# Copies of finished PSUM banks one step earlier, a strict turn of two banks, a fourth W_out step beside the attention units, and a new order at the loop's ends

## The chip, the core and the metric

The kernel runs on one NeuronCore of a Trainium2 chip. Its engines work in parallel, each through its own queue in order: TensorE (PE, with its weight loads as PEld), VectorE (DVE), ScalarE (ACT), GpSimd (POOL), and SyncE (SP), which here only starts DMAs. They wait for each other by semaphores. The metric is the device time of one execution in microseconds (us), the median of three runs.

## The reference

```python
scores = (q @ k.transpose(0, 1, 3, 2)) / sqrt(64)      # q, k, v: 8 batches x 8 heads x 576 x 64
scores = where(row // 64 >= col // 64, scores, -1e9)   # causal by blocks of 64
attn = exp(scores - max); attn = attn / (sum(attn) + 1e-9)
x = (attn @ v).transpose(0, 2, 1, 3).reshape(4608, 512)
h = x @ w_in                                           # 512 x 2048
out = (h * sigmoid(h)) @ w_out                         # 2048 x 512
```

## The kernel before

**Two halves of a number.** Inputs of the two FFN products are split into a rounded part ("hi", an ACT copy to fp32r) and a remainder ("lo", a subtraction), and each product is three fp32r matmuls. W_in and W_out arrive as 64-bit words and are turned into fp32 by hand: `load` (DMA), `rebias` (ACT), `bits:0` to `bits:2` (DVE). W_out has eight steps `t0` to `t7` of two half-steps each (`o0` to `o15`). A step then gets four ACT copies (`hi:0` to `hi:3`), three differences of its quarters (`x:0` to `x:2`) and four remainders (`lo:0` to `lo:3`). The first NTA steps go to a pool `ta` and leave `lo` and `x` to POOL alone; later ones use DVE for two `lo` and one `x`, and lie in pools that exist only when the attention's buffers have been given back (`all.attended`).

**The stages.** First (to about 80 us) the weights of W_in and the first two row blocks of the attention, in a packed form of their own. Then the loop: 64 units (batch, head), in 32 pairs `d0` to `d31`, with the remaining rows of the attention. Beside it run the steps of the first FFN product (`ffn1`), 160 in all, each into one PSUM bank `h`. After the loop the rest of them, then the second FFN product (`Item.prod`) until the end.

**A pair in the loop.** `run:0` and `run:1` interleave the scores of this pair with attn @ v of the pair two before (`score` and `pv`). The latter goes to two banks: `U` (`r` = 1) and one of the two banks of pool `pH`, where it is called `u` (`r` = 0). `half` (ACT, L795) copies `U` to SBUF, `fold` (DVE, L799) adds `u` to it and so frees `u`. POOL's `mult`, ACT's `x_hi` and POOL's `x_lo` make of it the input of later FFN steps. Then four FFN steps of two tokens `ffn` each take PE (L1067, 12 matmuls of 448 columns a step). Meanwhile DVE finds the maxima (`max`, L655, L704), their largest over partition groups goes through ACT's small copies (`gather`, `spread`) and DVE (`top`, `wide`), DVE subtracts (`sub`, L730, L733), ACT takes `exp` (L737), POOL adds up the row sums (`add`, L744 to L752), DVE reduces them (`sums`, L655 into `dj`), ACT gathers `dj` (`sums_g`, L664), POOL adds (`sums_m`, L808 to L812), and DVE inverts (`inverse`).

**The FFN's banks.** A step's bank `h` comes from `pH`, which has two buffers, and so do `u` and, later, two banks of the second product. A finished step is copied to SBUF by ACT (`keep`, L1073) and goes to DRAM by a DMA (`save`, L1078). The pool gives the next tile the buffer that, in the order below, is the first to be released.

**The order** of all this is written out by hand as a list of tokens, ORDER. Each token puts its instructions at the end of its engine's queue. `ffn`, `keep` and `save` take the next step of their own lists, so that a `keep` in the list belongs to the oldest step not yet copied. With steps counted, the tokens of one pair that concern PE and the banks read, where f81 is step 81, f81a and f81b its two halves, and K81 its copy:

```
d18.run:0 K79 d18.run:1 d16.half f81a d16.fold f81b f82a K80 f82b f83a K81 f83b f84a K82 f84b  d19.run:0 K83 ...
```

So K81 stands in the list behind the first half of step 83, two steps after its own.

Of the kernel before, what the change touches and what calls it, by code (L numbers as in the profile page):

```python
# [107 lines left out]
d0.fold t1.x:0 u5.load_v u8.load u9.load u5.max:0 d0.mult u4.top ffn u5.ones u5.max:1 u4.spread u5.max:2 d0.x_hi ffn u4.wide
keep d0.x_lo u5.gather u4.sub:0 save ffn t1.hi:1 u5.top u4.sub:1 u5.spread t1.x:1 u3.sums u4.exp:0 ffn u4.sub:2 t1.lo:1 keep
u5.wide d1.sums_g save u5.sub:2 ffn u4.exp:1 d1.sums_m u4.exp:2 u5.sub:0 u5.exp:2 u5.sub:1 d3.run:0 keep u4.add:0 d1.inverse  # L110
u5.exp:0 save u5.exp:1 u4.add:1 t1.hi:2 u4.add:2 d3.run:1 u4.add:3 d1.half u5.add:0 u4.sums u6.max:0 u5.add:1 ffn u6.max:1
u6.load_v u6.ones u7.load_v u10.load u11.load u6.max:2 u5.add:2 u5.add:3 ffn d1.fold u6.gather u7.max:0 d1.mult u6.top u7.ones
ffn u7.max:1 keep t1.x:2 u7.max:2 u6.spread save ffn u7.gather u6.wide d1.x_hi u6.sub:0 t1.hi:3 ffn d1.x_lo u7.top u6.sub:1 keep
u5.sums u7.spread save t1.lo:3 u6.sub:2 ffn d2.sums_g u7.wide u6.exp:0 d2.sums_m u7.sub:2 u6.exp:1 ffn keep u7.sub:0 u6.exp:2
u7.sub:1 u6.add:0 save ffn u7.exp:0 d2.inverse u7.exp:1 u6.add:1 u7.exp:2 d4.run:0 u6.add:2 keep u6.add:3 save u7.add:0 u6.sums
d4.run:1 d2.half u8.max:0 u7.add:1 u8.max:1 u8.ones u7.add:2 u8.max:2 u7.add:3 u8.gather ffn t1.lo:2 u8.load_v d2.fold u9.load_v
u12.load u13.load u9.max:0 d2.mult u8.top ffn u9.ones u9.max:1 u8.spread u9.max:2 d2.x_hi ffn u8.wide keep d2.x_lo u9.gather
u8.sub:0 save ffn u8.exp:0 u9.top u8.sub:1 u9.spread u7.sums u8.exp:1 ffn u8.sub:2 keep u8.add:0 u9.wide d3.sums_g save u9.sub:2
ffn u8.exp:2 d3.sums_m u9.sub:0 u9.exp:2 u9.sub:1 u9.exp:0 d5.run:0 u8.add:1 keep d3.inverse u9.exp:1 u8.add:2 save u8.add:3
u9.add:0 d5.run:1 u8.sums d3.half u10.max:0 u9.add:1 u10.max:1 u10.ones u10.max:2 u9.add:2 u9.add:3 u10.load_v d3.fold  # L120
u11.load_v u10.gather u14.load u15.load u11.max:0 d3.mult u10.top u11.ones u11.max:1 u10.spread u11.max:2 d3.x_hi u10.wide
u11.gather d3.x_lo u10.sub:0 u11.top u10.exp:0 ffn u10.sub:1 u11.spread u9.sums u10.exp:1 u10.sub:2 ffn d4.sums_g u10.add:0
u11.wide u10.exp:2 u11.sub:2 ffn keep d4.sums_m u11.sub:0 u11.exp:2 save u11.sub:1 ffn u11.exp:0 u11.exp:1 u10.add:1 d4.inverse
d6.run:0 u10.add:2 keep u10.add:3 save u11.add:0 u10.sums d6.run:1 d4.half u12.max:0 u11.add:1 u12.max:1 u12.ones u11.add:2
u12.max:2 u11.add:3 u12.gather ffn u12.load_v d4.fold u13.load_v u16.load u17.load u13.max:0 d4.mult ffn u12.top u13.ones
u13.max:1 u12.spread u13.max:2 ffn keep u12.wide u13.gather save ffn u12.sub:0 d4.x_hi u13.top u12.exp:0 d4.x_lo u12.sub:1 ffn
u13.spread u11.sums keep u12.sub:2 d5.sums_g ffn save u13.wide u12.exp:1 d5.sums_m u13.sub:2 u12.exp:2 ffn u13.sub:0 keep
u13.sub:1 u13.exp:0 u12.add:0 save ffn d5.inverse u13.exp:1 u13.exp:2 u12.add:1 d7.run:0 keep u12.add:2 save u12.add:3 u13.add:0
u12.sums d7.run:1 d5.half u14.max:0 u13.add:1 u14.max:1 u14.ones u13.add:2 u14.max:2 u13.add:3 u14.gather ffn u14.load_v d5.fold
u15.load_v u18.load u19.load u15.max:0 d5.mult ffn u14.top u15.ones u15.max:1 u14.spread u15.max:2 ffn keep u14.wide u15.gather  # L130
save ffn u14.sub:0 d5.x_hi u15.top u14.exp:0 d5.x_lo u14.sub:1 ffn u15.spread u13.sums keep u14.sub:2 d6.sums_g ffn save
u15.wide u14.exp:1 d6.sums_m u15.sub:2 u14.exp:2 ffn u15.sub:0 keep u15.sub:1 u15.exp:0 u14.add:0 save ffn d6.inverse u15.exp:1
u15.exp:2 u14.add:1 d8.run:0 keep u14.add:2 save u14.add:3 u15.add:0 u14.sums d8.run:1 d6.half u16.max:0 u15.add:1 u16.max:1
u16.ones u15.add:2 u16.max:2 u15.add:3 u16.gather ffn u16.load_v d6.fold u17.load_v u20.load u21.load u17.max:0 d6.mult ffn
u16.top u17.ones u17.max:1 u16.spread u17.max:2 ffn keep u16.wide u17.gather save ffn u16.sub:0 d6.x_hi u17.top u16.exp:0
d6.x_lo u16.sub:1 ffn u17.spread u15.sums keep u16.sub:2 d7.sums_g ffn save u17.wide u16.exp:1 d7.sums_m u17.sub:2 u16.exp:2 ffn
u17.sub:0 keep u17.sub:1 u17.exp:0 u16.add:0 save ffn d7.inverse u17.exp:1 u17.exp:2 u16.add:1 d9.run:0 keep u16.add:2 save
u16.add:3 u17.add:0 u16.sums d9.run:1 d7.half u18.max:0 u17.add:1 u18.max:1 u18.ones u17.add:2 u18.max:2 u17.add:3 u18.gather
ffn u18.load_v d7.fold u19.load_v u22.load u23.load u19.max:0 d7.mult ffn u18.top u19.ones u19.max:1 u18.spread u19.max:2 ffn
keep u18.wide u19.gather save ffn u18.sub:0 d7.x_hi u19.top u18.exp:0 d7.x_lo u18.sub:1 u19.spread u17.sums keep u18.sub:2 ffn  # L140
d8.sums_g save u19.wide u18.exp:1 d8.sums_m u19.sub:2 ffn u18.exp:2 u19.sub:0 u19.exp:2 u19.sub:1 d10.run:0 u19.exp:0 u18.add:0
d8.inverse keep u19.exp:1 save u18.add:1 u18.add:2 d10.run:1 u18.add:3 d8.half u19.add:0 u18.sums u20.max:0 u19.add:1 u20.max:1
ffn u20.ones u20.load_v u21.load_v u24.load u25.load u20.max:2 u19.add:2 u19.add:3 ffn d8.fold u20.gather u21.max:0 d8.mult ffn
u20.top u21.ones u21.max:1 keep u21.max:2 u20.spread save ffn d8.x_hi u20.wide u21.gather d8.x_lo ffn u20.sub:0 keep u21.top
u20.exp:0 u20.sub:1 save ffn u21.spread u19.sums u20.sub:2 d9.sums_g ffn u21.wide keep d9.sums_m u20.exp:1 u21.sub:2 save ffn
u20.exp:2 u21.sub:0 u21.exp:2 u20.add:0 u21.sub:1 u21.exp:0 d11.run:0 d9.inverse keep u20.add:1 u21.exp:1 save u20.add:2
u20.add:3 d11.run:1 d9.half u21.add:0 u20.sums u22.max:0 u21.add:1 u22.max:1 u22.ones u22.max:2 u21.add:2 ffn u22.load_v
u23.load_v u26.load u21.add:3 u27.load d9.fold u22.gather ffn u23.max:0 d9.mult u22.top u23.ones u23.max:1 ffn u22.spread
u23.max:2 keep u22.wide d9.x_hi ffn save u23.gather d9.x_lo u22.sub:0 ffn u23.top u22.exp:0 u22.sub:1 keep u21.sums u23.spread
# [1149 lines left out]
```

## Time and profile before

| | |
|---|---|
| Median of 3 runs | 1012.25 us (1011.24 to 1014.05) |
| The profiled execution | 1012.83 us, of which the span from the first to the last instruction is 1011.1 us |
| Mean granted TensorE clock | 0.992 |
| Busy: PE / PEld | 951.9 us (94%) / 825.5 us (82%) |
| Busy: DVE / ACT / POOL | 742.6 (73%) / 640.8 (63%) / 552.6 us (55%) |
| The chain that ended last | PE 74%, DVE 14%, ACT 6% |

How to read it: 59 us of the span are without PE. Which engine a stage waits for is not seen in shares of the whole span, but in the waits of that stage, and in what each engine does within one pair.

### The profile page before, as it was taken

What the parts mean: (1) busy time and instruction counts of PE and PEld (TensorE: products, weight loads), DVE (VectorE), ACT (ScalarE), POOL (GpSimd) and SP (SyncE); (2) the same over time, 40 slices, a digit from 0 to 9 for tenths busy, and PEclk for the clock granted to TensorE, in tenths of its full rate; (3) what the DMA queues carried; (4) which work ended last, traced back from release to release, by engine and by line L of the source; (5) the groups of instructions that cost most, each with busy time, mean ns of one, the idle gap of its engine ahead of it and who ended that gap; (6) DMA issues with size and microseconds to landing.
All of it is one profiled execution on the core that took longest, in us unless ns stands there. A gap on an engine that the chain in (4) does not pass through costs nothing.

```text
span 1011.1 us, 23797 instructions
## 1 busy us (share of the span) xinstructions
PE 951.9 (94%) x8730; PEld 825.5 (82%) x8730; DVE 742.6 (73%) x1518; ACT 640.8 (63%) x1621; POOL 552.6 (55%) x800
## 2 busy tenths in 40 slices
...
GB/s 353 369 170 135 113 97 113 101 116 122 99 130 103 115 120 98 128 98 132 144 118 116 81 61 198 203 205 127 172 163 132 152 137 126 159 132 134 144 81 42
DMA packets 109813, 139.97 MB, mean 138 GB/s; under 512 B 22656, under 2 KB 87168, under 8 KB 109696
## 3 DMA queue, kind: packets, MB, share of 16 engines
...
q8 instruction: 68, 1.11, 0.5%
...
HBM read 91.23 MB, written 47.19 MB: 137 GB/s over the span
## 4 chain that ended last, share of the span: by engine, by line
PE 74%; DVE 14%; ACT 6%; issue 2%; POOL 2%; DMA 1%; SPq 0%; DVEq 0%; ACTq 0%; POOLq 0%
PE h L1067 24%; PE c L1150 19%; PE S L1150 15%; PE u L791 6%; DVE Mx L655 6%; PE S L791 5%; PE SC L791 2%; DVE MR L659 2%; DVE xu L799 2%; ACT g L1073 2%; DVE p L730 2%; ACT m L722 2%; ACT p L737 1%; DMA p<-in_qk_dram 1%; DVE mj L704 1%
## 5 line engine op out<-in xcount | busy, mean ns | idle before, releaser
L1067 PE MATMUL h<-x,wi 128*128 128x448 f32 (+2 forms) x1968 | 425.6, 372 | 49.0 <-DVE xu L799 25.1
L1067 PEld LDWEIGHTS h<-x,wi 128*128 128x128 f32 x1968 | 361.2, 190 | 99.9 <-ACT g L1073 34.9
L1132 POOL TENSOR_TENSOR wi<-raw,wi 128x512 fp32r<-128x512 f32 (+1 forms) x114 | 115.9, 1030 | 148.2 <-ACT wi L1128 106.0
L1150 PE MATMUL c<-tb,wi 128*128 128x256 f32 x663 | 120.2, 276 | 0.0
L737 ACT ACTIVATE p<-p 128x448 f32<-128x448 f32 (+2 forms) x192 | 100.6, 572 | 7.5 <-DVE p L730 6.2
L1150 PEld LDWEIGHTS c<-tb,wi 128*128 128x128 f32 x663 | 102.0, 188 | 0.0
L791 PE MATMUL S<-qk 64*64 64x384 f32 (+1 forms) x512 | 98.6, 516 | 0.0
L1073 ACT COPY g<-h 128x448 f32<-128x448 f32 (+1 forms) x160 | 85.8, 536 | 17.6 <-PE h L1067 11.7
L655 DVE TRANSPOSE_TENSOR_REDUCE dj<-pa 128x14 f32<-128x448 f32 x64 | 40.6, 634 | 76.1 <-POOL pa L752 76.1
L1150 PE MATMUL S<-tb,wi 128*128 128x256 f32 x513 | 94.4, 276 | 0.0
L1095 ACT ACTIVATE raw<-raw 128x1024 f32<-128x1024 f32 x72 | 76.7, 1065 | 16.9 <-DMA raw<-gdb 10.1
L795 ACT COPY xb<-U 128x448 f32<-128x448 f32 x32 | 17.0, 532 | 107.8 <-PE U L791 107.8
L744 POOL TENSOR_TENSOR pa<-p 128x448 f32<-128x448 f32 x64 | 73.5, 1148 | 19.4 <-ACT p L737 12.5
L1150 PE MATMUL c<-ta,wi 128*128 128x256 f32 x519 | 83.8, 276 | 0.0
L747 POOL TENSOR_TENSOR pa<-pa,p 128x256 f32<-128x256 f32 (+1 forms) x128 | 78.1, 610 | 10.0
L791 PE MATMUL U<-p,v 64*64 64x64 f32 (+4 forms) x768 | 79.8, 354 | 0.0
L791 PE MATMUL u<-p,v 64*64 64x64 f32 (+4 forms) x768 | 78.4, 350 | 1.3 <-DVE xu L799 1.3
L1150 PEld LDWEIGHTS S<-tb,wi 128*128 128x128 f32 x513 | 79.2, 188 | 0.0
L1150 PEld LDWEIGHTS c<-ta,wi 128*128 128x128 f32 x519 | 73.3, 188 | 0.0
L730 DVE TENSOR_TENSOR p<-S,MR 128x448 f32<-128x448 f32 (+1 forms) x128 | 71.6, 581 | 1.1
L829 POOL TENSOR_TENSOR x<-xu,x 128x448 fp32r<-128x448 f32 x32 | 37.1, 1159 | 61.2 <-ACT x L826 59.6
L655 DVE TRANSPOSE_TENSOR_REDUCE Mx<-S 128x14 f32<-128x448 f32 (+1 forms) x128 | 69.2, 576 | 0.0
...
## 6 DMA issues: line engine op xcount, KB each, us to landing
gdb<-g SPq DMA_DIRECT2D x128, 224.0 KB, 2.0
...
```

What stands on the lines that cost most here:

```text
L655: nc.vector.tensor_reduce(out=out, in_=in_, axis=AX.X, op=op, apply_transpose=True)
L730: nc.vector.tensor_tensor(out=u.p[:, c : c + w], in0=s[:, :w], in1=u.mb[:, q : q + w], op=ALU.subtract)
L737: nc.scalar.activation(u.p[:, c : c + w], u.p[:, c : c + w], AF.Exp, scale=SCALE)
L744: nc.gpsimd.tensor_tensor(out=u.pa, in0=p[:, :NQ], in1=p[:, ZERO:COLS], op=ALU.add)
L747: nc.gpsimd.tensor_tensor(out=u.pa[:, q : q + w], in0=u.pa[:, q : q + w], in1=p[:, c : c + w], op=ALU.add)
L791: nc.tensor.matmul(o, w, x, start=start, stop=stop)
L829: nc.gpsimd.tensor_tensor(out=u.x[:, 1], in0=u.xu, in1=u.x[:, 0], op=ALU.subtract)
L1067: nc.tensor.matmul(o, w, x, start=half == 0 and i == 0 or f is None and i == 0, stop=(half == 1 or f is None) and i == len(runs) - 1)
L1073: nc.scalar.copy(g, hs.pop(z)[:, :n])
L1095: nc.scalar.activation(u.raw, u.raw, AF.Silu)
L1132: e.tensor_tensor(out=u.goal(1, k), in0=u.source(k), in1=u.goal(0, k), op=ALU.subtract)
L1150: nc.tensor.matmul(o[:, :HD], *runs[k], start=first, stop=u.q == 3 and n == 5, skip_group_check=True)
```

## The change

Nothing that is computed changes. Six edits:

- **Banks.** `pH` becomes two tiles with names of their own, and a new function takes them strictly in turn.
- **Copies.** From step 13 on the copy of each finished step (`keep`, and `save` behind it) stands one step earlier in the list: at every place where K79 stood, K80 stands now, and so on. The places themselves stay.
- **Buffers.** `half` copies straight into the tile that `fold` then adds to in place (tile `xb` is gone). The first NTA steps of W_out take their differences in place (no tile `xs`). The score tile is 64 columns shorter, and its strip of zeros is cleared before the first unit and no longer at the program's start.
- **A fourth W_out step beside the units.** NTA is 4. `t3` (with `o6`, `o7`) moves from behind the loop into the pairs d24 to d29, and `t2` (with `o4`, `o5`) from the pairs d23 to d31 to the pairs d17 to d24.
- **The loop's start.** The tokens of `t0`, `t1`, `o2`, `o3` are spread differently over pairs d0 to d4. Pairs d2 to d5 get three FFN steps each (before 3, 4, 3, 2), and the second half of step 32 changes places with the first half of step 33.
- **The loop's end.** Between the last two `run`s stand two FFN steps, where there was none, and behind `all.attended` come `o8` and `o9`.

```diff
-NTA = 3
+NTA = 4
-COLS = 1472
+COLS = 1408
-FOURS, TWOS, ONES, ZERO, WIDE = 448, 704, 832, 1024, 1088
+FOURS, TWOS, ONES, ZERO, WIDE = 448, 704, 832, 960, 1024
...
-    pH = pool("pH", bufs=2, space=PSUM)
+    pH = pool("pH", space=PSUM)
+    turns = [0]
+
+    def turn(name):
+        turns[0] += 1
+        return pH.tile([P, 512], F32, tag=f"h{turns[0] % 2}", name=name)
...
-    for t in PP:
-        nc.gpsimd.memset(t[:, ZERO:WIDE], 0.0)
...
-                u.sums = sp.tile([P, 4, 256], F32, tag="xs", name="xs")
-                e.tensor_tensor(out=u.sums[:, 0:2], in0=q[:, 1:4:2], in1=q[:, 0:2], op=sub)
+                if u.d < NTA:
+                    u.sums = [q[:, 0:2], q[:, 1:3]]
+                else:
+                    s = sp.tile([P, 4, 256], F32, tag="xs", name="xs")
+                    u.sums = [s[:, 0:2], s[:, 2:4]]
+                e.tensor_tensor(out=u.sums[0], in0=q[:, 1:4:2], in1=q[:, 0:2], op=sub)
...
+            if u.i == 0:
+                for t in PP:
+                    nc.gpsimd.memset(t[:, ZERO:WIDE], 0.0)
...
-            U = u.U[r] = pU.tile([P, 512], F32, tag="U", name="U") if r else pH.tile([P, 512], F32, tag="h", name="u")
+            U = u.U[r] = pU.tile([P, 512], F32, tag="U", name="U") if r else turn("u")
...
-            u.xb = sp.tile([P, NQ], F32, tag="xb", name="xb")
-            nc.scalar.copy(u.xb, u.U[1][:, :NQ])
+            u.xu = sp.tile([P, 512], F32, tag=f"xu{u.k % 2}", name="xu")[:, :NQ]
+            nc.scalar.copy(u.xu, u.U[1][:, :NQ])
...
-            u.xu = sp.tile([P, 512], F32, tag=f"xu{u.k % 2}", name="xu")[:, :NQ]
-            nc.vector.tensor_tensor(out=u.xu, in0=u.U[0][:, :NQ], in1=u.xb, op=ALU.add)
+            nc.vector.tensor_tensor(out=u.xu, in0=u.U[0][:, :NQ], in1=u.xu, op=ALU.add)
...
-            hs[z] = pH.tile([P, 512], F32, tag="h", name="h")
+            hs[z] = turn("h")
...
+    f = queues["ffn"]
+    f[65], f[66] = f[66], f[65]
```

Of ORDER, with the steps counted as above, a pair in the middle, and the loop's end:

```
before  d18.run:0 K79 d18.run:1 d16.half f81a d16.fold f81b f82a K80 f82b f83a K81 f83b f84a K82 f84b  d19.run:0 K83
after   d18.run:0 K80 d18.run:1 d16.half f81a d16.fold f81b f82a K81 f82b f83a K82 f83b f84a K83 f84b  d19.run:0 K84

before  d32.run:0 K135 d33.run:0 d30.half d30.fold f137a d31.half f137b K136 d31.fold f138 K137 all.attended o6.load o7.load
        o6.rebias o6.bits f139a o7.rebias K138 f139b ...
after   d32.run:0 K136 f137a d30.half d30.fold f137b f138a K137 f138b d33.run:0 K138 f139a d31.half d31.fold f139b f140a K139
        f140b K140 all.attended o8.load o9.load f141 f142a K141 o8.rebias f142b o9.rebias f143a K142 f143b ...
```

Where the new tokens of W_out stand in a pair: two or three `bits` behind `inverse`, ahead of `sums` (for `o4` and `o6` the third stands ahead of `fold`); `hi` on ACT ahead of `half`; `lo` and `x` on POOL ahead of `mult`, ahead of `x_lo` or ahead of `sums_m`.

## Rows read from the trace of the kernel before

**Rows 1.** PE's waits, 60 to 180 us: total us, times, longest us
```profile
PE h L1067 <- ACT g L1073: 5.7, 5, 3.1
```

**Rows 2.** PE's waits, 180 to 590 us
```profile
PE h L1067 <- DVE xu L799: 21.3, 26, 1.8
PE h L1067 <- ACT g L1073: 11.1, 22, 0.5
```

**Rows 3.** PE's waits, 590 to 620 us
```profile
PE h L1067 <- ACT g L1073: 5.3, 2, 3.1
PE u L791 <- DVE xu L799: 1.3, 1, 1.3
```

**Rows 4.** Windows: length, busy us of PE, PEld, DVE, ACT, POOL; clock, DMA
```profile
181.24:581.89 400.65, 369.23 (x3588) 289.46 (x3588) 305.82 (x631) 249.25 (x781) 260.69 (x457) 1.00 0.38 115
...
620.00:1011.10 391.10, 387.77 (x3249) 384.75 (x3248) 282.84 (x595) 263.52 (x495) 163.44 (x162) 1.00 0.49 142
```

**Rows 5.** Timeline of PE, pair d18: start, us, what, [idle before <-releaser]
```profile
367.01 0.59 PE L791 MATMUL S<-qk 64*64 64x448 f32 x2
...
372.56 5.08 PE L1067 MATMUL h<-x,wi 128*128 128x448 f32 x24 [0.76 <-DVE xu L799]
378.14 3.08 PE L1067 MATMUL h<-x,wi 128*128 128x448 f32 x14 [0.51 <-ACT g L1073]
```

**Rows 6.** Timeline of DVE, the same pair
```profile
368.04 0.65 DVE L655 TRANSPOSE_TENSOR_REDUCE dj<-pa 128x14 f32<-128x448 f32 x1 [2.62 <-POOL pa L752]
369.55 0.72 DVE L655 TRANSPOSE_TENSOR_REDUCE Mx<-SC 128x16 f32<-128x512 f32 x1 [0.87 <-PE U L791]
...
371.88 0.62 DVE L799 TENSOR_TENSOR xu<-u,xb 128x448 f32<-128x448 f32 x1 [0.23 <-PE u L791]
...
376.98 0.62 DVE L655 TRANSPOSE_TENSOR_REDUCE dj<-pa 128x14 f32<-128x448 f32 x1
...
384.18 0.65 DVE L655 TRANSPOSE_TENSOR_REDUCE dj<-pa 128x14 f32<-128x448 f32 x1 [2.61 <-POOL pa L752]
```

**Rows 7.** Timeline of ACT, the same pair
```profile
369.61 0.53 ACT L795 COPY xb<-U 128x448 f32<-128x448 f32 x1 [3.66 <-PE U L791]
...
374.31 0.53 ACT L1073 COPY g<-h 128x448 f32<-128x448 f32 x1
...
377.56 0.53 ACT L1073 COPY g<-h 128x448 f32<-128x448 f32 x1
378.12 0.66 ACT L664 COPY dj<-dj 32x28 f32<-32x28 f32 x3
```

**Rows 8.** Timeline of POOL, the same pair
```profile
378.86 0.30 POOL L808 TENSOR_TENSOR rt<-dj 32x56 f32<-32x56 f32 x1 [1.49 <-DVE MR L659]
...
383.17 0.98 POOL L752 TENSOR_TENSOR pa<-pa,p 64x128 f32<-64x128 f32 x2
```

**Rows 9.** Timeline of DVE, pair d10, behind a pair with three FFN steps
```profile
242.59 0.67 DVE L655 TRANSPOSE_TENSOR_REDUCE Mx<-SC 128x16 f32<-128x512 f32 x1
...
256.52 0.65 DVE L655 TRANSPOSE_TENSOR_REDUCE dj<-pa 128x14 f32<-128x448 f32 x1 [2.34 <-POOL pa L752]
```

**Rows 10.** Timeline of DVE, between pairs d27 and d28, with W_out work
```profile
527.55 1.11 DVE L563 SCALAR_TENSOR_TENSOR wraw<-wst,wraw 128x512 uint32<-128x512 uint32 x1
```

**Rows 11.** Timeline of POOL, the same pair
```profile
527.31 1.67 POOL L747 TENSOR_TENSOR pa<-pa,p 128x256 f32<-128x256 f32 x2
```

**Rows 12.** Timeline of DVE, first maximum of pairs d2 and d6
```profile
114.74 0.72 DVE L655 TRANSPOSE_TENSOR_REDUCE Mx<-SC 128x16 f32<-128x512 f32 x1 [0.38 <-PE U L791]
...
179.00 0.72 DVE L655 TRANSPOSE_TENSOR_REDUCE Mx<-SC 128x16 f32<-128x512 f32 x1 [3.20 <-PE U L791]
```

**Rows 13.** Timeline of PE at the loop's end
```profile
601.86 9.07 PE L1067 MATMUL h<-x,wi 128*128 128x448 f32 x36 [2.25 <-ACT g L1073]
...
613.98 10.27 PE L1067 MATMUL h<-x,wi 128*128 128x448 f32 x36 [3.06 <-ACT g L1073]
```

**Rows 14.** Windows, as rows 4, right behind the second of these stalls
```profile
614.00:616.00 2.00, 2.00 (x5) 1.80 (x6) 1.86 (x3) 0.84 (x2) 0.73 (x1) 0.50 0.61 154
```

More of the change, by code (lines that the diff above doesn't have):

```diff
@@ L108 @@
[L108 to L149, printed above, removed]
@@ L166 @@
-d15.run:1 d13.half u30.max:0 u29.add:1 u30.max:1 u30.ones u29.add:2 u30.max:2 u29.add:3 u30.gather ffn u30.load_v d13.fold
-u31.load_v u34.load u35.load u31.max:0 d13.mult ffn u30.top u31.ones u31.max:1 u30.spread u31.max:2 ffn keep u30.wide u31.gather
-save ffn u30.sub:0 d13.x_hi u31.top u30.exp:0 d13.x_lo u30.sub:1 ffn u31.spread u29.sums keep u30.sub:2 d14.sums_g ffn save
-u31.wide u30.exp:1 d14.sums_m u31.sub:2 u30.exp:2 ffn u31.sub:0 keep u31.sub:1 u31.exp:0 u30.add:0 save ffn d14.inverse
@@ new lines @@
+t1.hi:1 u3.add:0 u2.sums d2.run:1 d0.half u4.max:0 u3.add:1 u4.max:1 u4.ones u3.add:2 u4.max:2 u3.add:3 u4.gather ffn u4.load_v
+d0.fold t1.lo:0 u5.load_v u8.load u9.load u5.max:0 u4.top ffn d0.mult u5.ones u5.max:1 u4.spread u5.max:2 t1.lo:1 d0.x_hi ffn
+u4.wide keep u4.sub:0 u5.gather d0.x_lo save ffn u4.exp:0 u5.top u4.sub:1 t1.x:0 u5.spread u3.sums ffn u4.exp:1 u4.sub:2 keep
+u4.add:0 u5.wide d1.sums_g save ffn u5.sub:2 u4.exp:2 d1.sums_m t1.hi:2 u5.sub:0 u5.exp:2 u5.sub:1 d3.run:0 u4.add:1 keep
@@ new lines @@
+d1.inverse u5.exp:0 save u4.add:2 u5.exp:1 u4.add:3 d3.run:1 u5.add:0 d1.half u4.sums u6.max:0 u5.add:1 u6.max:1 u6.ones
+u6.max:2 u5.add:2 ffn u5.add:3 u6.load_v u7.load_v d1.fold u10.load u11.load u6.gather u7.max:0 d1.mult ffn u6.top u7.ones
+u7.max:1 u6.spread t1.lo:2 u7.max:2 d1.x_hi ffn u6.wide keep d1.x_lo u7.gather u6.sub:0 save ffn t1.x:1 u7.top u6.exp:0 u6.sub:1
+u7.spread u5.sums t1.x:2 ffn u6.exp:1 u6.sub:2 keep u7.wide u6.add:0 d2.sums_g save ffn u7.sub:2 u6.exp:2 d2.sums_m u7.sub:0
@@ new lines @@
+u7.exp:2 u7.sub:1 d4.run:0 u7.exp:0 keep u6.add:1 d2.inverse u7.exp:1 save u6.add:2 t1.hi:3 u6.add:3 d4.run:1 d2.half u7.add:0
+u6.sums u8.max:0 u7.add:1 u8.max:1 u8.ones u8.max:2 ffn u7.add:2 u8.load_v u9.load_v u12.load u7.add:3 u13.load d2.fold
+u8.gather u9.max:0 ffn d2.mult u8.top u9.ones u9.max:1 u8.spread t1.lo:3 u9.max:2 ffn keep u8.wide u9.gather save ffn u8.sub:0
+d2.x_hi u9.top u8.exp:0 d2.x_lo u8.sub:1 u9.spread u7.sums ffn keep u8.sub:2 d3.sums_g save u9.wide ffn u8.exp:1 d3.sums_m
@@ new lines @@
+u9.sub:2 u8.exp:2 u9.sub:0 u9.exp:2 d5.run:0 u9.sub:1 keep u8.add:0 d3.inverse u9.exp:0 save u9.exp:1 u8.add:1 u8.add:2 d5.run:1
+d3.half u8.add:3 u9.add:0 u8.sums u10.max:0 ffn u9.add:1 u10.max:1 u10.load_v u10.ones u11.load_v u14.load u15.load u10.max:2
+u9.add:2 u9.add:3 ffn d3.fold u10.gather u11.max:0 d3.mult u10.top u11.ones ffn u11.max:1 keep u11.max:2 u10.spread save ffn
+u11.gather u10.wide d3.x_hi u10.sub:0 d3.x_lo u11.top u10.exp:0 u10.sub:1 u11.spread u9.sums u10.exp:1 ffn u10.sub:2 d4.sums_g
@@ new lines @@
+u10.add:0 u11.wide u10.exp:2 ffn u11.sub:2 keep d4.sums_m u11.sub:0 u11.exp:2 save d6.run:0 u11.sub:1 keep u11.exp:0 u10.add:1
+save d4.inverse u11.exp:1 u10.add:2 u10.add:3 d6.run:1 d4.half u11.add:0 u10.sums u12.max:0 u11.add:1 u12.max:1 u12.ones ffn
+u12.max:2 u11.add:2 u12.load_v u13.load_v u16.load u17.load u11.add:3 d4.fold u12.gather ffn u13.max:0 d4.mult u12.top u13.ones
+u13.max:1 ffn u12.spread u13.max:2 keep u12.wide ffn d4.x_hi save u13.gather d4.x_lo u12.sub:0 ffn u13.top keep u12.sub:1
@@ new lines @@
+u32.load_v d14.fold u33.load_v u36.load u37.load u33.max:0 d14.mult ffn u32.top u33.ones u33.max:1 u32.spread u33.max:2 ffn keep
+u32.wide u33.gather save ffn u32.sub:0 d14.x_hi u33.top u32.exp:0 d14.x_lo u32.sub:1 ffn u33.spread u31.sums keep u32.sub:2
+d15.sums_g ffn save u33.wide u32.exp:1 d15.sums_m u33.sub:2 u32.exp:2 ffn u33.sub:0 keep u33.sub:1 u33.exp:0 u32.add:0 save ffn
+d15.inverse u33.exp:1 u33.exp:2 u32.add:1 d17.run:0 keep u32.add:2 save u32.add:3 u33.add:0 u32.sums d17.run:1 d15.half
@@ new lines @@
+u34.add:1 d18.run:0 keep u34.add:2 save u34.add:3 o5.load u35.add:0 u34.sums d18.run:1 d16.half u36.max:0 u35.add:1 u36.max:1
+u36.ones u35.add:2 u36.max:2 u35.add:3 u36.gather ffn u36.load_v d16.fold u37.load_v u40.load u41.load o4.rebias u37.max:0
+d16.mult ffn u36.top u37.ones u37.max:1 u36.spread u37.max:2 ffn keep u36.wide u37.gather save ffn u36.sub:0 d16.x_hi u37.top
+u36.exp:0 d16.x_lo u36.sub:1 ffn u37.spread u35.sums keep u36.sub:2 d17.sums_g ffn save u37.wide u36.exp:1 d17.sums_m u37.sub:2
@@ new lines @@
+u36.exp:2 ffn u37.sub:0 keep u37.sub:1 u37.exp:0 u36.add:0 save ffn d17.inverse u37.exp:1 u37.exp:2 o4.bits:0 u36.add:1
+d19.run:0 keep o4.bits:1 u36.add:2 save u36.add:3 u37.add:0 u36.sums d19.run:1 d17.half u38.max:0 u37.add:1 u38.max:1 u38.ones
+u37.add:2 u38.max:2 u37.add:3 o4.bits:2 u38.gather ffn u38.load_v u39.load_v u42.load d17.fold u43.load u39.max:0 d17.mult ffn
+u38.top u39.ones u39.max:1 u38.spread ffn u39.max:2 keep u38.wide d17.x_hi save ffn u39.gather d17.x_lo u38.sub:0 o5.rebias
@@ new lines @@
+u40.add:2 t2.hi:0 save u40.add:3 t2.hi:1 u41.add:0 u40.sums d21.run:1 d19.half u42.max:0 u41.add:1 u42.max:1 u42.ones u41.add:2
+u42.max:2 u41.add:3 u42.gather ffn u42.load_v d19.fold u43.load_v u46.load t2.lo:0 u47.load u43.max:0 ffn u42.top u43.ones
+d19.mult u43.max:1 u42.spread u43.max:2 ffn keep t2.lo:1 u42.wide u43.gather save ffn u42.sub:0 d19.x_hi u43.top u42.exp:0
+d19.x_lo u42.sub:1 ffn u43.spread u41.sums keep u42.sub:2 t2.x:0 d20.sums_g ffn save u43.wide u42.exp:1 d20.sums_m u43.sub:2
@@ new lines @@
+u42.exp:2 ffn u43.sub:0 keep u43.sub:1 u43.exp:0 u42.add:0 save ffn d20.inverse u43.exp:1 u43.exp:2 u42.add:1 t2.hi:2 d22.run:0
+u42.add:2 keep u42.add:3 save u43.add:0 u42.sums d22.run:1 d20.half u44.max:0 u43.add:1 u44.max:1 u44.ones u43.add:2 u44.max:2
+u43.add:3 u44.gather ffn u44.load_v d20.fold u45.load_v u48.load t2.lo:2 u49.load u45.max:0 ffn u44.top u45.ones d20.mult
+u45.max:1 u44.spread u45.max:2 ffn keep t2.x:1 u44.wide u45.gather save ffn u44.sub:0 d20.x_hi u45.top u44.exp:0 d20.x_lo
```

498 lines of the change are left out of this document (252 added, 246 removed).

## The prediction, made before the changed kernel was run

> **What bounds the kernel now.** I read the waits of PE first, cut by stage. Behind the loop PE is all but full: 387.8 us busy of 391.1 [rows 4], so nothing is to be had there. Before, PE waits for two things. In 180 to 590 us it waits 26 times for the fold of a pair (21.3 us) and 22 times for ACT's copy of a finished bank (11.1 us) [rows 2]. In 60 to 180 us the copies alone cost it 5.7 us [rows 1], and at the loop's end both together 6.6 us [rows 3].
>
> Then one pair, engine by engine. PE starts `run:0` at 367.01, ends `run:1` at 371.80, waits 0.76 for the fold, runs two steps in 5.08 (2.54 each), waits 0.51 for a copy, and runs two more [rows 5]. So the step right behind the runs has been given the bank of `u`, which the fold must empty first: DVE gets `u` whole at 371.88 and is done at 372.50 [rows 6]. And the third step takes the first one's bank: that was finished at 375.1, but ACT copies it only at 377.56, two places later in its queue [rows 5, 7]. The period is 16.15, and PE works 16.15 - 0.76 - 0.51 = 14.88 of it.
>
> Could the other engines go faster than 16.15? DVE idles 0.87 for PE before its first maximum, 0.23 for PE before the fold, and 2.6 for POOL's sums [rows 6]. The circle that does not pass through PE is this: first maximum at 369.55, sums of the odd unit at 376.98, ACT's gather of `dj` at 378.12, POOL's small sums from 378.86, its adds to 384.15, DVE's `dj` to 384.83, and the next maximum [rows 6 to 8]. That is 15.28, and without the 0.23 for PE 15.05. One place of the trace shows it without PE: behind a pair with three steps DVE goes on with no wait at 242.59 and is through `dj` at 257.17, 14.58 later [rows 9], in a slightly different order of ACT's queue. So this circle runs at some 15.05, hardly slower than PE's 14.88.
>
> **The change, part by part.**
>
> *Turn and copies.* No instruction is added. With two banks strictly in turn, the step behind the runs takes the bank of the fourth step before them, whose copy now stands behind `run:0`, where ACT otherwise waits 3.66 us for PE [rows 7]. The second step takes `u`'s bank: in the frame of rows 5 it starts at 374.34, the fold is done at 372.50, so there are 1.84 us to spare. The third step starts at 376.88 and needs the copy of the first, which ACT reaches at 374.31 and can start at 374.34. The fourth starts at 379.42 and needs the copy that ACT reaches at 377.56 [rows 7]. Both waits go. What is late next is the circle above: 15.05 instead of 16.15.
>
> Behind a copy in ACT's queue stand the odd unit's gather and `dj`'s gather. A copy that must wait for its own step would hold them up: for the first by 0.03, for the second not at all (that step ends at 376.88). I take nothing.
>
> *A fourth W_out step in the loop.* It brings two loads, two rescalings and four roundings on ACT, six bit operations on DVE, three differences and four remainders on POOL. ACT's roundings stand ahead of `half`, within those 3.66 us, and each is about as long as a copy of a bank, 0.53 [rows 7]. POOL's fall into its waits ahead of `mult`, `x_lo` and the small sums; the last of these is 1.49 [rows 8], and if it were full each us more would be a us of the circle. DVE's stand mostly in the 2.6 us before `dj`. There they are not free: such an operation took 1.11, and the two POOL adds beside it 1.67 [rows 10, 11], where adds otherwise lie on the circle. The plain length of the pair of adds is not in these rows; I take 0.4 us for each half-step `o4` to `o7`, and 0.7 for the two operations ahead of a fold (between nothing, if the 1.84 covers them, and 1.11): 4 x 0.4 + 2 x 0.7 = 3.0. Of this DVE may once fall behind PE by the 1.84 that the fold has to spare, which leaves 1.2.
>
> The Trainium skill has a rule on this, in SBUF — State Buffer, "Who interferes with whom": a DVE instruction with two SBUF inputs contends with a GpSimd instruction that reads SBUF, and the one that comes second waits. The trace agrees with it: that bit operation reads two SBUF tiles, and it took 1.11 beside the add [rows 10]. By the rule every one of these operations that meets an add would hold up one or the other; that is a rival below.
>
> *The loop, summed.* From 181.24 to 581.89 there are 25 periods in 400.65 us [rows 4]. 25 x 15.05 + 1.2 = 377.5, a gain of 23.2. Bounds: PE alone, 369.2 [rows 4], a gain of 31.4; and 25 x 15.28 with 1.11 for each of four half-steps, 386.4, a gain of 14.2.
>
> *The loop's start.* From pair d2 to d6 it is 64.26 us between first maxima [rows 12]. PE's work there is spread over the pairs as 3, 3, 3, 3 steps, and the circle bounds it: 4 x 15.05 = 60.2, a gain of 4.1. Before d2, PE waits for copies: 5.7 less the 3.1 of the longest, which lies later, so at most 2.6 [rows 1]. I take 1.9. Together 6.0, between 3 (half of it) and 8.5 (4 x 14.58 for the circle, and all 2.6).
>
> *The loop's end.* Two FFN steps between the last runs (5.08) cover the fold, which DVE did 0.7 after the runs in the regular pair, and ACT's copies of finished steps no longer stand behind both `half`. Behind `all.attended` the copy that the rescalings hold up (they wait for their load) has the bank of a step two later; before it was needed at once. So 6.6 of waits go [rows 3]. The two long ones cost more than themselves: 36 matmuls took 9.07 and 10.27 behind them [rows 13], where 24 take 5.08 and so 36 take 7.62. Behind the second the granted clock is 0.50, its 1.2 GHz level [rows 14], after PE had idled 3.06 us; in the regular pairs, with stalls under 1 us, it is 1.00 [rows 4]. That is 1.45 + 2.65 = 4.1 more. Of 10.7 I take 10.3; if one wait for the new loads stays with its slow clock, 6.
>
> *The rest.* `half` and `fold` do the same copy and the same addition on other tiles. Differences in place need the copies and remainders of a quarter first, which the order has. The strips of zeros are cleared by POOL before the first unit, where it waits for weights; if that cover is gone they cost at most four times the 0.62 of a fold, 2.5 us. I take nothing for these.
>
> *Sum.* 23.2 + 6.0 + 10.3 = 39.5. The profiled execution took 1012.83, so 973.3; it stands 0.58 above the median of the runs, so 972.7, and I say **973**.
>
> **The rivals.**
>
> *The fold's wait only moves* (if the fold comes too late for the second step as well). Then only copies' waits go: 5.7 + 11.1 + 5.3 and the 4.1 of clock, 26.2, which gives 986. For it speaks that the fold stands behind three maxima in DVE's queue; against it the 1.84 us to spare.
>
> *W_out's operations and POOL's adds hold each other up* (the rule above). Three operations for each of four half-steps, of which two read two SBUF tiles: eight that cost up to the 1.11 of rows 10 each, 8.9 in place of 3.0, so 979. Rows 10 and 11 speak for it; against it that before the change two of the half-steps were in the loop already.
>
> *Slower: ACT's early copies block ACT.* If a copy finds its step unfinished and waits through it, 2.54 us, the odd unit's chain behind it in the queue goes on that much later: 15.05 + 2.54 = 17.6 a pair, 25 x 1.45 = 36 us lost against the 16.3 won at the ends, so 1032. It decides from 1.75 us of such waiting a pair ((16.15 - 15.05) + 16.3 / 25). Rows 7 give 0.03.
>
> *No change.* If the pool gave the banks as before whatever their names, the early copies alone would change nothing at the fold, and the circle could eat the rest: 1012. The names speak against it, for a tile's name is its bank.
>
> **How the numbers follow.** The forecast has 0.72, the moved fold 0.10, the mutual hold-up 0.10, slower 0.04, no change 0.04. The forecast's own bounds: all high gains, 31.4 + 8.5 + 10.7 = 50.6, give 961; all low ones, 14.2 + 3 + 6 = 23.2, give 989. 961 to 990 holds the first three cases, 0.92, of which I leave some for sizes that I have not seen. A measurement of this kernel can tell about 0.3% (3 us) from no change; by that, faster has 0.92, same 0.04, slower 0.04.
>
> **What would show it.** In the changed profile PE should have no wait for a fold or a copy above 0.3 us in a regular pair; its period should be 14.9 to 15.3, and DVE's wait for PE before the first maximum should be all but gone while its 2.6 for POOL stays. At the loop's end no matmul should run at 0.50 of the clock. Behind the loop nothing should move. The prediction is wrong if the second step behind the runs waits for the fold, if ACT shows waits for PE ahead of its copies of a us or more, or if POOL's adds grow in the pairs with W_out work by more than 1 us each.

## The result, and the profile after

The kernel after takes **963.8 us** (963.1 to 963.9), the kernel before 1012.4 beside it: ratio 0.952 (95% interval 0.950 to 0.953). The forecast was 973, within 961 to 990. The profiled spans differ by 49.0 us (1011.1 and 962.1), where the forecast's terms make 39.5.

By the marks of the prediction (DVE's first maximum of a pair, and the first matmul of the second product):

| stretch | before | after | gain | forecast |
|---|---|---|---|---|
| start to d2 | 114.74 | 112.72 | 2.0 | 1.9 |
| d2 to d6 | 64.26 | 57.19 | 7.1 | 4.1 |
| d6 to d31 | 400.65 | 372.45 | 28.2 | 23.2 |
| d31 to the first product | 85.23 | 73.30 | 11.9 | 10.3 |
| the products, to the end | 346.2 | 346.4 | -0.2 | 0 |

(About 1.0 of the first row is chance: PE waits 2.19 us for the first load of `qk` in the trace of before and 1.19 in that of after, but 1.07 in e3 below, whose start is that of before.)

From the page of after, PE's busy time and the chain that ended last:

```profile
PE 945.1 (98%) x8730; PEld 823.9 (86%) x8730; DVE 735.1 (76%) x1515; ACT 641.4 (67%) x1621; POOL 558.9 (58%) x803
...
PE 46%; DVE 20%; POOL 17%; ACT 8%; issue 5%; DMA 2%; SPq 0%; POOLq 0%; DVEq 0%; ACTq 0%
```

PE is busier, and yet its share of the chain fell from 74% to 46%, while DVE and POOL rose. That is the first sign that another engine now sets the time of the loop. PE's waits after, for 60 to 170, 170 to 550 and 550 to 620 us (total us, times, longest), which answer to [rows 1 to 3]:

```profile
PE h L1077 <- POOL x L839: 0.7, 1, 0.7
PE h L1077 <- ACT g L1083: 0.6, 2, 0.3
...
PE h L1077 <- DVE xu L809: 2.4, 5, 0.7
PE h L1077 <- ACT g L1083: 2.3, 6, 0.5
PE U L802 <- DVE p L744: 0.6, 1, 0.6
...
PE h L1077 <- ACT g L1083: 1.3, 1, 1.3
PE h L1077 <- DVE xu L809: 0.2, 1, 0.2
```

Of 32.4 us in the loop 5.3 are left, of 6.6 at its end 1.5. The windows of the loop, of the products and of one plain pair, d17 (length, busy us of PE, PEld, DVE, ACT, POOL; clock, DMA), beside [rows 4]:

```profile
169.91:542.36 372.45, 367.23 (x3592) 290.32 (x3588) 305.03 (x639) 252.47 (x786) 270.79 (x465) 1.00 0.42 126
615.66:962.00 346.34, 343.08 (x3025) 342.88 (x3023) 253.85 (x551) 234.78 (x443) 143.92 (x143) 1.00 0.47 134
331.65:346.40 14.75, 14.75 (x152) 11.68 (x147) 11.85 (x26) 9.93 (x31) 10.13 (x19) 1.00 0.61 177
```

The clock is at its upper level, 1.00, in these stretches. That pair on DVE's timeline, against [rows 6]:

```profile
331.65 0.67 DVE L663 TRANSPOSE_TENSOR_REDUCE Mx<-SC 128x16 f32<-128x512 f32 x1
...
333.62 0.61 DVE L809 TENSOR_TENSOR xu<-u,xu 128x448 f32<-128x448 f32 x1
...
338.72 0.62 DVE L663 TRANSPOSE_TENSOR_REDUCE dj<-pa 128x14 f32<-128x448 f32 x1
...
345.83 0.65 DVE L663 TRANSPOSE_TENSOR_REDUCE dj<-pa 128x14 f32<-128x448 f32 x1 [2.57 <-POOL pa L763]
346.40 0.68 DVE L663 TRANSPOSE_TENSOR_REDUCE Mx<-SC 128x16 f32<-128x512 f32 x1
```

and on ACT's, against [rows 7]:

```profile
336.04 0.53 ACT L1083 COPY g<-h 128x448 f32<-128x448 f32 x1
...
339.24 0.54 ACT L1083 COPY g<-h 128x448 f32<-128x448 f32 x1
339.80 0.66 ACT L672 COPY dj<-dj 32x28 f32<-32x28 f32 x3
...
341.44 0.52 ACT L1083 COPY g<-h 128x448 f32<-128x448 f32 x1
```

And PE's four steps of that pair, where [rows 5] had two waits:

```profile
332.41 10.10 PE L1077 MATMUL h<-x,wi 128*128 128x448 f32 x48
```

In this pair DVE waits for PE neither ahead of the first maximum nor ahead of the fold; its 2.57 for POOL stays. The circle of the prediction reads here: 7.07 to the odd unit's sums, 1.08 to the gather, 6.03 through POOL to the even unit's sums, 0.57 to the next maximum: 14.75. PE seems to need 14.75 as well. Which of the two holds the period is for the experiments.

### The profile page after: what moved, and what is told of

The parts are those of the page before. It is cut to its first block, busy times and chain, and to the rows that moved or that the text cites. A ratio compares the mean times of both kernels' runs of the same rounds, so it can differ in the third digit from the quotient of the medians.

```text
span 962.1 us, 23795 instructions
## 1 busy us (share of the span) xinstructions
PE 945.1 (98%) x8730; PEld 823.9 (86%) x8730; DVE 735.1 (76%) x1515; ACT 641.4 (67%) x1621; POOL 558.9 (58%) x803
## 4 chain that ended last, share of the span: by engine, by line
PE 46%; DVE 20%; POOL 17%; ACT 8%; issue 5%; DMA 2%; SPq 0%; POOLq 0%; DVEq 0%; ACTq 0%
PE c L1160 20%; PE S L1160 16%; DVE Mx L663 9%; PE h L1077 8%; POOL pa L758 4%; POOL pa L755 4%; POOL pa L763 3%; POOL rs L822 3%; DVE dj L663 2%; ACT m L733 2%; ACT g L1083 2%; DVE MR L667 2%; ACT dj L672 2%; DVE xu L809 2%; DVE p L741 2%
## 5 line engine op out<-in xcount | busy, mean ns | idle before, releaser
L1077 PE MATMUL h<-x,wi 128*128 128x448 f32 (+2 forms) x1968 | 417.5, 368 | 7.9 <-ACT g L1083 4.2
L1077 PEld LDWEIGHTS h<-x,wi 128*128 128x128 f32 x1968 | 356.1, 188 | 53.4 <-ACT g L1083 11.6
L1083 ACT COPY g<-h 128x448 f32<-128x448 f32 (+1 forms) x160 | 85.7, 536 | 20.1 <-PE h L1077 14.8
L1160 PE MATMUL c<-ta,wi 128*128 128x256 f32 x684 | 87.0, 276 | 0.0
L1160 PEld LDWEIGHTS c<-ta,wi 128*128 128x128 f32 x684 | 81.9, 188 | 0.0
L1160 PE MATMUL c<-tb,wi 128*128 128x256 f32 x498 | 81.4, 276 | 0.0
L719 ACT COPY Mx<-Mx 64x4 f32<-64x4 f32 x128 | 24.7, 193 | 81.4 <-DVE Mx L663 79.8
L1160 PEld LDWEIGHTS c<-tb,wi 128*128 128x128 f32 x498 | 71.0, 188 | 0.0
L1160 PE MATMUL S<-ta,wi 128*128 128x256 f32 x534 | 70.2, 276 | 0.0
L802 PEld LDWEIGHTS u<-p,v 64*64 64x64 f32 x768 | 43.9, 133 | 28.2 <-issue 23.2
L1160 PEld LDWEIGHTS S<-ta,wi 128*128 128x128 f32 x534 | 65.0, 188 | 0.0
```

Of the source, the lines that this page charges most:

```text
L802: nc.tensor.matmul(o, w, x, start=start, stop=stop)
L1077: nc.tensor.matmul(o, w, x, start=half == 0 and i == 0 or f is None and i == 0, stop=(half == 1 or f is None) and i == len(runs) - 1)
L1083: nc.scalar.copy(g, hs.pop(z)[:, :n])
L1160: nc.tensor.matmul(o[:, :HD], *runs[k], start=first, stop=u.q == 3 and n == 5, skip_group_check=True)
```

## Experiments

**1. Which edit does it?** Three kernels: the copies alone, the turn alone, and after without the turn.

```diff
# e1: before, ORDER: one copy more at d0, one fewer at the loop's end
-d0.run:0 u3.load ...           d31.x_lo keep save all.attended
+d0.run:0 keep save u3.load ... d31.x_lo all.attended
# e2: before, two named banks (K136 stands ahead of d33.run:0)
-    pH = pool("pH", bufs=2, space=PSUM)
+    pH = pool("pH", space=PSUM)
+    def turn(name): ...
# e8: after, the pool picks
-        return pH.tile([P, 512], F32, tag=f"h{turns[0] % 2}", name=name)
+        return pH.tile([P, 512], F32, tag="h", name=name)
```

> The kernel before, its banks still picked by the pool, with one edit: from step 13 on each copy of a finished step stands one place earlier in the list, so that K80 stands where K79 stood (at the loop's end one copy fewer follows, and the rest is as before). If the place of the copies does the work and the names do not matter, the pool itself finds a copied bank for the step behind the runs: pairs d6 to d31 take 25 x 14.75 and some 2 us for the half-steps o4 and o5, 371, a gain of about 29 there and of 2 to 4 ahead of it; the loop's end stays as before; about 980 us in all. If the strict turn is needed (the pool would go on giving that step the bank of u), the fold's 21 us of waits stay and only the copies' 11 to 17 go: 996 to 1001. If neither alone does anything: 1012.

Measured: 966.2 us, ratio 0.955 (0.953 to 0.957). From d6 to d31 370.56 us, ahead of d6 171.2 (before 179.0), and even the loop's end is 9.4 shorter, where I expected nothing. PE's waits of e1 from 170 to 550 us:

```profile
PE h L1067 <- ACT g L1073: 1.6, 4, 0.5
PE h L1067 <- DVE xu L799: 0.8, 2, 0.5
```

The fold's 21 us of waits are gone with the pool still picking. Once the copy of the fourth step stands behind `run:0`, that bank is the first to come free, and the pool gives it to the step behind the runs by itself. e1 has 46 of the 48.6 us; all other edits together, the fourth W_out step among them, are worth some 2.4.

> The kernel after, with the two banks left to the pool to pick (one name, two tiles) in place of the strict turn; all else as after. If the early copies alone decide, the pool picks the same banks: within 1 us of after, 963 to 965. If the turn is what frees the step behind the runs from the fold, that wait comes back, some 0.7 us a pair: about 981.

Measured: 964.7 us (964.0 to 964.7), ratio 0.953 (0.951 to 0.955); from d6 to d31 372.40 beside 372.45 of after. The turn does nothing here.

> The kernel before with the two banks strictly in turn and the copies where they were (one copy, K136, is set ahead of the last run, without which the turn would block itself). If turn and copies only work together, the step behind the runs now waits for a copy that ACT reaches only behind both gathers of the next unit: in the frame of the pair shown it would start at about 374.8 in place of 372.56, the wait for the fold and the one for the third step go, and the period is 16.15 + 3.0 - 0.76 - 0.51 = 17.9, 25 x 1.75 = 44 us more: about 1055. If the turn alone frees the step from the fold: 0.76 a pair less, about 990. If names change nothing: 1012.

Measured: 1109 us at a mean granted clock of 0.936, and 1127 at 0.915. The profile is of the second, and what follows is read from it alone. A pair takes 20.48 instead of my 17.9. PE's timeline and ACT's in one of its pairs, and the window of its four FFN steps:

```profile
370.15 12.65 PE L1072 MATMUL h<-x,wi 128*128 128x448 f32 x48 [3.12 <-ACT g L1078]
```

```profile
369.57 0.53 ACT L1078 COPY g<-h 128x448 f32<-128x448 f32 x1
```

```profile
370.15:382.74 12.59, 12.59 (x49) 11.23 (x49) 7.13 (x14) 7.04 (x19) 6.82 (x13) 0.76 0.35 117
```

The wait for the late copy is 3.12, as worked out (3.0). The rest is the clock: behind such a stall it is at a mean of 0.76 through the four steps (0.50, the 1.2 GHz level, from 370.15 to 376 us, and 1.00 from 378 on), and they take 12.65 instead of 10.1. 17.9 + 2.55 = 20.45. So the copies alone bring the gain, and the turn without them loses about 100 us.

**2. Is PE or the circle the bound of a pair?** Less work for PE in one kernel, a shorter circle in the other.

```diff
# e4: the third product of the batch's FFN steps left out
-for k, (wt, xt) in enumerate(((0, 0), (0, 1), (1, 0))):
+for k, (wt, xt) in enumerate(((0, 0), (0, 1), (1, 0))[: 3 if f is None else 2]):
# e5: two of POOL's four additions of a unit left out
             elif k < 3:
+                return
```

> The kernel after, with the third product (low part of the weights by high part of x) left out of the FFN steps of the batch: 16 of 48 matmuls of a pair, some 3.4 us of PE's 14.75, are gone; all else as after. PE then can't bound a pair, and the period shows the circle that does not pass through PE. By my sum of before it is 15.05 and would not get shorter than the 14.75 already seen, so 14.75 in a plain pair, with 3.4 us of idle PE. If PE is what holds the pairs at 14.75, the period falls below it, at the lowest to DVE's 11.85 busy; between them the circle's own length, by its parts in the pair shown of after (7.07 + 1.82 + 5.25 + 0.61) at most 14.75.

Measured: 960.7 us; plain pairs 14.72 to 14.75, as in after, and PE's waits from 180 to 550 us (total us, times, longest):

```profile
PE h L1077 <- ACT g L1083: 35.3, 46, 1.3
PE h L1077 <- DVE xu L809: 25.6, 25, 2.2
```

A third fewer FFN matmuls change nothing in the loop (372.02 from d6 to d31), and DVE waits for PE ahead of no first maximum there: the circle holds the pairs at 14.74.

> The kernel after, with two of a unit's four additions on POOL left out (those of the scores by fours and by twos), 1.26 us for each unit, which lie on the circle that does not pass through PE; PE's work is all there. If the circle bounds the pairs, a plain one gets 1.2 us shorter than 14.75, about 13.5, which PE with 14.75 busy could not follow; so if PE bounds as well, plain pairs stay at 14.75 and only the pairs with W_out's operations lose their extra 0.3 to 1.6: about 4 us in the loop, 959 in all. If PE's 14.75 is stretched by waits hidden in its matmuls, the period falls to between 14 and 14.6, 945 to 960.

Measured: 948.9 us; plain pairs 14.53. The window of one, and DVE's timeline in it:

```profile
307.20:321.73 14.53, 14.53 (x148) 11.76 (x144) 12.05 (x26) 10.04 (x31) 7.83 (x14) 1.00 0.42 125
```

```profile
320.51 0.65 DVE L663 TRANSPOSE_TENSOR_REDUCE dj<-pa 128x14 f32<-128x448 f32 x1 [1.35 <-POOL pa L764]
321.73 0.72 DVE L663 TRANSPOSE_TENSOR_REDUCE Mx<-SC 128x16 f32<-128x512 f32 x1 [0.57 <-PE U L803]
```

Now DVE waits for PE again: PE alone needs 14.53. Of the cases that I had named it is the third that held, 14 to 14.6, with waits hidden in PE's matmuls. The 14.75 busy of after hid a wait of 0.22 a pair. It is not in PE's rows but in those of its weight loads, 331 to 347 us of after:

```profile
PEld h L1077 <- ACT g L1083: 0.3, 1, 0.3
```

That is the copy at 339.24, which stands in ACT's queue, and ACT is part of the circle.

**3. The circle put to the test.** If it bounds, taking one copy out of it must bring PE's 14.53 with all work in place.

```diff
# e10: after, ORDER, in 18 of the pairs d7 to d30
-u35.spread u33.sums keep u34.sub:2 d16.sums_g ffn save
+u35.spread u33.sums u34.sub:2 d16.sums_g keep ffn save
```

> The kernel after with one move in 18 of the pairs d7 to d30: ACT's gather of the sums stands ahead of the third copy of a bank instead of behind it. The two runs before say that the circle through DVE, ACT and POOL holds a plain pair at 14.75 and PE alone would take 14.53. The gather now starts when DVE has the odd unit's sums and not behind a copy of 0.53: the circle gets some 0.45 shorter, 14.3, and PE bounds: 14.53 a plain pair, 18 x 0.22 = 4.0 us, about 959.5. If the 14.53 of the run with fewer additions came from the missing additions and PE can't do better than 14.75 beside the full ones: no change, 963.8. If the copy, now 0.7 later, is late for the bank: PE shows a wait for it in each pair, and the period stays or grows.

Measured: 959.95 us, ratio 0.9505 (0.9491 to 0.9519); from d6 to d31 368.60, 3.85 less than after. In a plain pair ACT's gather and copy, PE's four steps, and the window:

```profile
532.60 0.66 ACT L672 COPY dj<-dj 32x28 f32<-32x28 f32 x3 [0.15 <-DVE dj L663]
533.17 0.52 ACT L1083 COPY g<-h 128x448 f32<-128x448 f32 x1
```

```profile
526.69 9.88 PE L1077 MATMUL h<-x,wi 128*128 128x448 f32 x48
```

```profile
524.67:539.20 14.53, 14.53 (x148) 11.75 (x144) 11.84 (x26) 9.93 (x32) 10.10 (x19) 1.00 0.27 90
```

14.53, as forecast from the two runs before (14.3 to 14.4 behind a long pair, where DVE catches up), and the copy is not late. PE holds the pair by way of ACT, whose first copy of a bank, at 529.40, waits 0.15 for its step; in the pair shown of after no copy waits. That the total came out at the 4.0 forecast is partly luck: pair d24 grew by 1.8 (part 6), and the others gave 5.6.

**4. What W_out's operations cost, and where.**

```diff
# e6: the bit operations of o4 to o7 left out
         def bits(u, j):
+            if u.kind == "out" and 2 <= u.d < 4:
+                return
# e7: after, ORDER (o6.bits:2 and o7.bits:2 likewise go to the gap around d27.run:0, t3.hi:0 behind them)
-u37.add:3 o4.bits:2 u38.gather ...  u41.exp:2 o5.bits:2 u40.add:1
+u37.add:3 u38.gather ...            u41.exp:2 o4.bits:2 o5.bits:2 u40.add:1
-o8.rebias ffn o8.bits:0 o9.rebias ffn o8.bits:1 keep save
+ffn keep save o8.rebias o8.bits:0 o9.rebias ffn o8.bits:1
```

> The kernel after, with the bit operations of the half-steps o4 to o7 left out (12 operations on DVE; W_out's values are then wrong, their rescalings, roundings and remainders are all there). By the profile of after the pairs with these operations take 0.33 to 1.62 us more than the plain 14.75, 4.5 in all; if DVE's operations are the cause, all pairs take 14.75 and the kernel is 4 to 4.5 us faster, 959.5. By my forecast's 1.2 it would be 962.5. If the rescalings on ACT and the remainders on POOL are the cause, nothing changes: 963.8.

Measured: 958.6 us, ratio 0.948 (0.946 to 0.949); from d6 to d31 367.25, 5.2 less than after. Of this 4.6 lie in the five pairs that hold these 12 operations (d18, d19, d20, d24, d25): 0.39 each. The rest lies mostly in plain pairs, which take 14.71 to 14.74 here and nearly the same in e4 and e7, where the operations are in place. DVE's timeline of after beside such operations, and POOL's:

```profile
358.59 1.10 DVE L567 SCALAR_TENSOR_TENSOR wraw<-wst,wraw 128x512 uint32<-128x512 uint32 x1
360.98 0.65 DVE L663 TRANSPOSE_TENSOR_REDUCE dj<-pa 128x14 f32<-128x448 f32 x1 [1.29 <-POOL pa L763]
...
363.52 0.97 DVE L573 SCALAR_TENSOR_TENSOR wraw<-wst,wraw 128x512 uint32<-128x512 uint32 x1
364.40 0.61 DVE L809 TENSOR_TENSOR xu<-u,xu 128x448 f32<-128x448 f32 x1
```

```profile
358.35 1.66 POOL L758 TENSOR_TENSOR pa<-pa,p 128x256 f32<-128x256 f32 x2
```

In the gap ahead of the sums the operation costs what it takes from POOL's pair of adds (1.66 here, 1.26 in plain pairs: 0.4, the sum's term), ahead of the fold its whole 0.97.

> The kernel after with two moves in the list. The last bit operations of o4, o6 and o7 leave their places ahead of a fold (or as a third in one pair) for the gap in which DVE waits for POOL ahead of the sums, in pairs with one or two of them; and at the loop's end copy K142 stands ahead of the rescalings of o8 and o9. If an operation ahead of a fold costs more than one in the gap, the two long pairs (+1.28 and +1.62) fall to +0.4: 2 us; and the wait of 1.32 at the loop's end goes: 960.5 in all. If an operation costs the same wherever it stands, only the 1.3: 962.5. If the copy ahead of the rescalings holds these up in turn: 963.8.

Measured: 961.3 us, ratio 0.950 (0.949 to 0.952), from d6 to d31 370.51, 1.94 less than after: the two long pairs fell from 16.03 and 16.37 to 14.98 and 14.99, and two others grew by 0.3 and 0.6. At the loop's end PE's one wait fell from 1.32 to 0.66.

**5. The loop's end before.**

```diff
# e3: before, ORDER
-all.attended o6.load o7.load o6.rebias ... o7.rebias keep o6.bits:2 save
+keep save all.attended o6.load o7.load o6.rebias ... o7.rebias o6.bits:2
```

> The kernel before with one copy (K138, the one that stood behind the rescaling of o7, which waits for its load) moved ahead of both rescalings at the loop's end. My theory: the second long stall of PE (3.06 us) goes, and with it the stretch at the 1.2 GHz clock behind it, 2.65 us: 5.7 less, 1006.5. If the slow clock has another reason than that stall: 3.1 less, 1009.3, and matmuls at 0.50 stay. If the wait only moves to the next step, which needs the bank after: 1012.

Measured: 1012.7 us, ratio 1.001 (1.000 to 1.002): nothing. PE's timeline, and ACT's, against [rows 13]:

```profile
601.86 2.68 PE L1067 MATMUL h<-x,wi 128*128 128x448 f32 x12 [2.25 <-ACT g L1073]
605.19 7.49 PE L1067 MATMUL h<-x,wi 128*128 128x448 f32 x36 [0.65 <-DVE xu L799]
617.09 23.25 PE L1067 MATMUL h<-x,wi 128*128 128x448 f32 x107 [4.41 <-ACT g L1073]
```

```profile
613.25 0.66 ACT L536 ACTIVATE wraw<-wst 128x512 f32<-128x512 f32 x1 [4.81 <-DMA wst<-in_moe_w_out_dram]
```

The stall of 3.06 moved to the next copy behind the rescalings and became 4.41. What holds up PE is the load, which ACT waits for; any copy behind it will do. In e1, with the old order at the loop's end and each copy one step earlier, the two stalls are 1.55 and 1.29:

```profile
562.40 2.67 PE L1067 MATMUL h<-x,wi 128*128 128x448 f32 x12 [1.55 <-ACT g L1073]
569.25 48.49 PE L1067 MATMUL h<-x,wi 128*128 128x448 f32 x240 [1.29 <-ACT g L1073]
```

So the earlier copies do most of it there; the two steps more that after puts ahead of the loads were not run alone. The clock behind the stall of 2.25, in the windows of before and of e3 (as rows 4):

```profile
602.00:606.00 4.00, 4.00 (x14) 3.61 (x15) 1.40 (x3) 0.00 (x0) 2.04 (x7) 0.62 0.16 57
602.00:606.00 4.00, 3.35 (x16) 2.79 (x17) 1.39 (x3) 0.00 (x0) 2.05 (x7) 1.00 0.16 57
```

**6. All moves together.** e9 joins e7 and e10 and sets K143 ahead of `t4.hi:0`; e11 also issues the loads of `o6` and `o7` one pair earlier.

> All the moves together: the gather ahead of the copy in 18 pairs, W_out's last bit operations out of the places ahead of a fold, copy K142 ahead of the rescalings and K143 ahead of the first rounding of t4 at the loop's end. If they add up: 961.3 less 4.0 less the 0.66 that PE still waits at the loop's end: 956.6; and pairs with W_out's operations lose less than 0.3 each, since the circle has 0.2 to spare. If the gather's place brings nothing: 960.6.

Measured: 958.3 us, ratio 0.949 (0.947 to 0.950), 366.62 from d6 to d31. That is 1.7 above the 956.6 that all moves add up to. The pairs with W_out's operations still take 15.0 to 15.1, 0.5 above the plain 14.53 and not less than 0.3. PE's wait at the loop's end did not go: it is 0.55, for K145, which stands behind the rescaling of `o10` as in e7. And one pair, d24, took 16.33 (17.05 in e10): with the pairs shorter, a load comes too late. ACT's timeline of e10:

```profile
447.25 0.69 ACT L540 ACTIVATE wraw<-wst 128x512 f32<-128x512 f32 x1 [1.48 <-DMA wst<-in_moe_w_out_dram]
449.23 0.53 ACT L1083 COPY g<-h 128x448 f32<-128x448 f32 x1 [1.29 <-DMA gdb<-g]
```

> All the moves together, and the two loads of o6 and o7 one pair earlier in the list. In the run with all moves one pair took 16.33: ACT waited there 1.21 us for the load of o6 at its rescaling, and then 1.24 for the store of a bank's copy whose tile the next copy needs. If the late load is what makes that pair long (the store runs beside the same loads), the pair falls to 14.4 to 15: 1.4 to 1.9 us, about 956.6. If the store's wait has another reason and alone makes it: no change, 958.3.

Measured: **956.7 us**, ratio 0.9455 (0.9437 to 0.9472), a span of 954.8 and 365.51 from d6 to d31; that pair took 15.03. ACT's wait for the load is gone there; its wait for the store is still 1.2, so the load made the pair long. This is the fastest version, 7 us below after, and its interval lies below that of after (0.950 to 0.953).

## Why the prediction held, step by step

- **Turn and copies.** Both waits went, as forecast. But the step that gave the fold's wait to the strict turn was wrong: e1 and e8 show that the early copies do all of it, and the rival "no change" asked about names that decide nothing. With the early copies the second step has the bank of `u`, and DVE's fold is done in time; that part was right. The forecast was for both edits at once, so this error left no mark on its number.
- **The circle, 15.05 a pair: right in kind, 0.30 too long.** e4 shows that it bounds, at 14.74. I read it at 15.28 from a pair in which PE still made DVE wait, and took off only 0.23. From the first maximum to the odd sums it is 7.07, not 7.20; the way on to the gather is 0.06 shorter and POOL's 0.03; and 0.08 are that I added the whole of the last sums, whose successor starts 0.57 after them. 25 x 0.30 = 7.5 us of gain that I left out.
- **PE's 14.88: too long by 0.35.** I took the period less the two waits that its rows showed. e5 and e10 give 14.53. The lower bound of the loop, 369.2, was wrong with it: e11 takes 365.5.
- **W_out's 1.2: too small.** It costs 4.6 (e6). The 3.0 of my sum counted the gap's operations by POOL's 0.4; ahead of a fold an operation costs 1.05 (e7, 16.03 to 14.98), not 0.7. And the 1.84 that the fold has to spare against PE paid for nothing, since DVE itself lies on the circle. POOL's adds beside such an operation took 1.66 in place of 1.26. This is the mark in the trace of the Trainium skill's rule (SBUF — State Buffer, "Who interferes with whom"). The 8.9 of the rival was too much.
- **The loop's sum.** 25 periods of 14.75 are 368.75, and the loop of after is 3.7 longer: 4.15 in the five pairs with W_out's operations and 0.4 in others (0.35 in d15, as long without these operations), less 0.9 in pairs that are shorter, d6 to d12. The 3.7 are 2.5 more than the 1.2; and 23.2 + 7.5 - 2.5 = 28.2. The circle and W_out missed in opposite directions, which brought the total nearer: that is luck.
- **The loop's start, 6.0:** it is 9.1 with the shorter first load, 8 without. Pairs with three steps take 14.0 to 14.8 there, not 15.05. And I counted PE's waits for copies alone: from 60 to 180 us it also waits 3.8 for the fold, four times, which rows 1 leave out. Of these 9.5 us of waits 0.6 are left. The copies alone give 6.5 of it from d0 to d6 (94.98 to 88.47 in e1), the new order the other 1.4 (87.08).
- **The loop's end, 10.3:** it is 11.9. The waits and the slow clock went as forecast. I had put it down to the new order there, but e1, with the old order, has 9.4 of it. The cause of the slow clock behind the stall of 2.25 stays open: in e3 the same stall left the clock at 1.00. The executions of before have mean clocks from 0.990 to 0.997, so the 1.45 that I took for that stretch rests on one profile and may not be in every execution.
- **Nothing behind the loop:** right, 346.2 and 346.4.
- **The signs named in advance:** in a regular pair no wait of PE above 0.3 (it is 0.22, hidden), DVE's wait for PE gone, no 1.2 GHz at the loop's end, POOL's adds longer by 0.4 and not by 1, no copy of ACT's waiting for PE between 170 and 542 us: all held. Only the period, 14.75, lies below the 14.9 to 15.3.
